# A gated mix of a state-space scan and a long convolution: pair 7 in the plain form, a tile of pair 6 ahead of the last inverse, two of C's sums by DMA, the last row by halves

## The chip, the cores and the metric

The kernel runs on one core of one Trainium2 chip. The metric is device time in microseconds of one execution, as the median of several runs. A core has TensorE (PE, matrix products into PSUM), VectorE (DVE), ScalarE (ACT), GpSimd (POOL) and SyncE (SP), each with its own queue of instructions that it takes in order; DMA transfers are issued from the queues of SP and POOL (a few at the start from ACT) and run on 16 shared DMA engines. An engine waits for another, or for a transfer, on semaphores.

## The reference

Inputs are in bfloat16: a sequence x of 2048 rows and 1024 columns, a diagonal complex state model (1024 states), k and v of the same shape as x, a four-tap filter and a long filter of 2048 taps for each column.

```python
def _A_ref(x, Lambda_re, Lambda_im, B_re, B_im, C_re, C_im, log_dt, Dskip):
    Lam_bar = jnp.exp(dt * Lam)
    B_bar = ((Lam_bar - 1.0) / Lam)[:, None] * Bmat
    Bu = jnp.einsum("bld,pd->blp", x + 0j, B_bar)
    ...
    for t in range(L):
        h = Lam_bar[None, :] * h + Bu[:, t, :]
    ...
    y = 2.0 * jnp.einsum("blp,dp->bld", hseq, Cmat).real + x * Dskip[None, None, :]

def _B_ref(q, k, v, shift_k, ssm_k, ssm_D):
    for t in range(ks):
        k_shift = k_shift + k_pad[:, t:t + S, :] * shift_k[:, ks - 1 - t][None, None, :]
    kv = k_shift * v
    ...
    y_f = kv_f * kf_f[None, :, :, :]
    ...
    y = y + kv * ssm_D[None, None, :]
    return q * y
...
g = _sigmoid((x * gate_w).sum(-1, keepdims=True))
a = _A_ref(x, Lambda_re, Lambda_im, B_re, B_im, C_re, C_im, log_dt, Dskip)
b = _B_ref(x, B_k, B_v, B_shift_k, B_ssm_k, B_ssm_D)
return g * a + (1 - g) * b
```

`kv_f` and `kf_f` are transforms of kv and of the long filter, padded to 4096; `y` is transformed back and cut to 2048 rows, a causal convolution along the sequence.

## The kernel before

**Two halves that overlap.** The first part, to about 212 us, is the convolution. It goes over eight channels c (128 columns each): the four taps and the product with v, transforms of the filter and of kv as matmuls with cosine and sine tables (`fwd_K`, `fwd_V`), their products on VectorE (`products`, tile G), and the transform back (`inverse`: two halves of 8 matmuls into `psz`, each copied by ScalarE to `cv` and stored by SP to a scratch in DRAM, `cv_scr`). In the last channel (lines 1088 to 1116) `products` sums on VectorE alone.

The second part is the state model. Time is cut into 4 blocks tb of 512 rows, the states into 4 groups g of 256 (two sub-groups j of 128). A *pair* i is one (tb, g), in the order of the list `order` (line 671): pairs 4 and 5 are (2, 0) and (2, 1), pair 6 is (0, 2), pair 7 is (0, 3), pair 8 is (1, 2), and so on. For each pair `Bu(i)` makes two tiles, one for each j. The scans then run over pairs of time steps: an even-step input V and an odd-step input U, where V must also hold lam (the complex pole) times the input of the step before.

**Two forms of a tile.** `Bu_tile` (line 710) makes 16 matmuls of 256 columns for the odd steps (`odd`), copies them to U on ScalarE, 16 for the even steps (`even`), and then, after a `yield`, adds lam times the shifted odd steps into the same PSUM with four matmuls against diagonal matrices (`lamd`, made by `lam_diag` from six scaled copies of the identity); for tb > 0 four matmuls of one column are added. `Bu_plain` (line 736) makes 16 matmuls of 512 columns (`both`) for odd and even steps at once and copies them out as they are; `turn_U` (line 750) then adds lam times the shifted odd steps in two parts: ScalarE scales into a tile Q (2 instructions of 512 columns in the first part, 4 of 256 in the second), and a DMA issued by POOL adds Q into V (`gather`). Both parts add into the same V, so the second sum is issued only after the first has landed. Pairs 4, 5 and 8 to 15 are plain; pairs 0 to 3, 6 and 7 have diagonal products.

**The scans and C.** `scan` (line 761) does one pair on VectorE: A from the table times U's V part, two sums, four scan instructions W, hb from W (the even states), then U += lam * hb (the odd states). `advance(j)` runs scan j and already starts scan j + 1 within it. Each of the eight tiles CT of C (`turn_C`, line 1070) must be turned by a complex factor: ScalarE makes two scaled copies m (`m<-CT`), VectorE scales CT twice and adds m (`CT<-CT,m`, 2048 columns). They are done in pairs after scans 0 to 3: CT0 and CT1, CT2 and CT3, and so on.

An output row tile t (128 rows of the output) is `Cy`: for g = 0 to 3, `Cy_g` (line 850) makes 8 matmuls of 512 columns into two PSUM banks, the left and right halves dh of the 1024 columns; rows 0 and 1 of a block read hb, rows 2 and 3 read U. `psy` is the PSUM tile. The convolution's row is loaded from `cv_scr` (`pbb`), scaled by 1 - g on ScalarE, summed with g times Dskip by a DMA of POOL (`pbb<-gd`), multiplied with x on VectorE (`product`), and added to the scaled state part by another DMA (`combine`) or, in the last four rows, on VectorE (`finish`). Row 15 is finished in two halves of 512 columns.

**What sets the order.** Every engine's order is the order in which the program records its instructions (`put` chains each to the one before it on its engine). So generators and lists written out by hand set it: `step(gen)` records the next piece of a generator; `plan` (line 1162) says which tiles of `Bu` (`B8`) and which rows (`C0`) stand behind each scan; `turned` (line 1163) says behind which scan `turn_U` of a pair is recorded; `on_act` holds scalings of CT that are slipped in between tiles. PSUM has four buffers of two banks (`tag="ps"`), used in turn, so a tile of matmuls needs the copies of the fourth tile before it to be done. Pool `Q` has four buffers. DMA transfers of one queue are issued in order, so a store that waits on ScalarE holds back the loads recorded behind it.

Around the change the order on TensorE is: both tiles of pairs 4 and 5 and the gate of block 2, tile 0 of pair 6 (odd, even), first half of the last inverse, tile 0's diagonal products, second half of the inverse, tile 1 of pair 6, the tiles of pair 7, then B8 to B12 and the first row C0.

Of the kernel before, what the change touches and what calls it, by code (L numbers as in the profile page):

```python
# [9 lines left out]
ALU = mybir.AluOpType  # L10
ACT = mybir.ActivationFunctionType
BF16 = mybir.dt.bfloat16
# [8 lines left out]
def kernel(  # L21
# [26 lines left out]
    nc = tc.nc  # L48
# [4 lines left out]
    S, D = xf.shape  # L53
# [5 lines left out]
    NT = S // 128  # L59
# [8 lines left out]
    def pool(name, bufs, **kw):  # L68
        return ctx.enter_context(tc.tile_pool(name=name, bufs=bufs, **kw))
# [6 lines left out]
    lam_pool = pool("lam", 1)  # L76
# [3 lines left out]
    s5p = {"wu": pool("wu", 3)}  # L80
    psum = pool("psum", 4, space=bass.MemoryType.PSUM)

    def u4(shape, dt, name):
        return s5p["wu"].tile(shape, dt, name=name, tag="u4")

    def ps2(shape, name):
        return psum.tile(shape, F32, name=name, tag="ps")
# [4 lines left out]
    def put(eng, f, *a, **kw):  # L92
        with tc.issue_after(prev[eng]) if eng in prev else nullcontext():
            i = f(*a, **kw)  # L94
        prev[eng] = getattr(i, "ins", i)

    def mm(o, l, r, first, last):
        put("pe", nc.tensor.matmul, o, lhsT=l, rhs=r, start=first, stop=last)
# [6 lines left out]
    def tt(o, a, b, op):  # L105
        put("dve", V.tensor_tensor, out=o, in0=a, in1=b, op=op)

    def ts(o, a, s1, s2, op0, op1=None):
        if op1 is None:
            put("dve", V.tensor_scalar, out=o, in0=a, scalar1=s1, scalar2=None, op0=op0)  # L110
        else:
            put("dve", V.tensor_scalar, out=o, in0=a, scalar1=s1, scalar2=s2, op0=op0, op1=op1)
# [4 lines left out]
    def act(o, i, **kw):  # L117
        put("act", nc.scalar.activation, out=o, in_=i, **kw)
# [7 lines left out]
    def gather(o, i):  # L126
        put("pool", nc.gpsimd.dma_start, out=o, in_=i, accum_op=ALU.add)
# [111 lines left out]
    def flat(ap):  # L239
        return ap.rearrange("p a b -> p (a b)")  # L240
# [100 lines left out]
    def small(name):  # L341
        return consts.tile([128, NP], F32, name=name)

    rv, rv2, thn, nthn = small("rv"), small("rv2"), small("thn"), small("nthn")
    c2r, mc2r, mc2i = small("c2r"), small("mc2r"), small("mc2i")
# [303 lines left out]
    def gates_of(c4, sums):  # L649
        act(gcols[:, c4], sums, func=ACT.Sigmoid)  # L650
        act(omg[:, c4], sums, func=ACT.Sigmoid, scale=-1.0)

    def gate(tb):
        psg = ps2([128, 2, 512], "p")[:, 0, 0:4]
        for tl in range(4):
            for dt_ in range(ND):
                mm(psg[:, tl:tl + 1], xTs[tb][:, dt_, tl * 128:(tl + 1) * 128], gwb[:, dt_:dt_ + 1],
                   dt_ == 0, dt_ == ND - 1)
        gates_of(slice(tb * 4, tb * 4 + 4), psg)
# [15 lines left out]
    def lam_diag(g, home, on_act=False):  # L675

        t = lamd[g] = home.tile([128, 2, 3, 128], BF16, name=f"lamd{g}", tag=f"lamd{g % 2}")
        for j in range(2):
            for k, f in enumerate((lam[:, 0], lam[:, 1], mlam)):
                pi = 2 * g + j  # L680
                if on_act:
                    act(t[:, j, k], ident, func=ACT.Identity, scale=f[:, pi:pi + 1])
                else:
                    ts(t[:, j, k], ident, f[:, pi:pi + 1], None, ALU.mult)

    def Bu(i):
        tb, g = order[i]
        if i in (10, 11):
            if i == 10:
                s5p["u2"] = xt_pool.tile([128, 2, 2 * (4 * HB + 4)], BF16, name="U2", tag="xT")  # L690
            U = s5p["u2"][:, i - 10]
        else:
            shape = [128, 2 * (4 * HB + 4)]
            if i in (6, 7, 8, 15):
                U = u4(shape, BF16, "U")
            else:
                home = uu[0 if i in (0, 1, 13, 14) else 1] if i < 6 or i in (13, 14) else s5p["uu"]
                U = home.tile(shape, BF16, name="U")
        if i in (4, 5) or i >= 8:
            V_, O_ = U[:, 0:4 * HB], U[:, 4 * HB:]  # L700
            V_ = V_.rearrange("p (c j t) -> p c j t", c=2, j=2)
            O_ = O_.rearrange("p (c j t) -> p c j t", c=2, j=2)
            Us[tb, g] = V_, O_[:, :, :, 2:]
            turns_U[i] = turn_U(g, V_, O_)
            return [Bu_plain(tb, g, V_, O_, j) for j in range(2)]
        U = U[:, 0:8 * HB].rearrange("p (a c j t) -> p a c j t", a=2, c=2, j=2)
        Us[tb, g] = U[:, 0], U[:, 1]
        return [Bu_tile(tb, g, U, j, (i, j) == (2, 1)) for j in range(2)]
# [26 lines left out]

    def Bu_plain(tb, g, V_, O_, j):
        xT = xTs[tb]
        if j == 0:
            act(O_[:, :, :, 1], ends[:, 1 - tb % 2, g], func=ACT.Copy)
        ps = ps2([128, 2, 2, HB], "both")  # L740
        for c in range(2):
            for dt_ in range(ND):
                mm(flat(ps[:, c]), BT[g][:, c, dt_, j * 128:(j + 1) * 128], xT[:, dt_], dt_ == 0, dt_ == ND - 1)
        act(O_[:, :, j, 2:], ps[:, :, 1], func=ACT.Copy)
        if j == 1 and tb < NTB - 1:
            act(ends[:, tb % 2, g], O_[:, :, :, HB + 1], func=ACT.Copy)
        act(V_[:, :, j], ps[:, :, 0], func=ACT.Copy)
        yield

    def turn_U(g, V_, O_):  # L750
        both = slice(0, 2)
        for part in (((both, both, lam[:, 0]),), ((0, 1, lam[:, 1]), (1, 0, mlam))):
            Q = s5p["Q"].tile([128, 2, 2, HB], BF16, name="Q")
            for j in range(2):
                pi = 2 * g + j
                for c, o, f in part:
                    act(Q[:, o, j], O_[:, c, j, 1:1 + HB], func=ACT.Identity, scale=f[:, pi:pi + 1])
            gather(V_, Q)
            yield
# [90 lines left out]
    def Cy_g(tb, tl, ps, g, last):  # L850
        X = hbs[tb, g] if tl < 2 else Us[tb, g][1]
        tsl = slice(tl % 2 * 128, tl % 2 * 128 + 128)
        for j in range(2):
            for c in range(2):
                for dh in range(2):
                    mm(ps[dh], X[:, c, j, tsl], CT[2 * g + j][:, c, dh * 512:(dh + 1) * 512],
                       g == 0 and j == 0 and c == 0, last and j == 1 and c == 1)

    def a_room(t_):
        if t_ < NT - 8:  # L860
# [43 lines left out]
    def step(gen):  # L904
        next(gen, None)

    def run(gen):
        for _ in gen:
            pass

    def steps(gen, n):
        for _ in range(n):
            step(gen)
# [141 lines left out]
    c = NC - 1  # L1055
    CT = {}
# [11 lines left out]
    m_pool = pool("m", 2, side="right")  # L1068

    def turn_C(pi):  # L1070
        m = m_pool.tile([128, 2, D], BF16, name="m")
        for c in range(2):
            act(m[:, c], CT[pi][:, 1 - c], func=ACT.Identity, scale=mc2i[:, pi:pi + 1])
            yield
        for c, f in enumerate((c2r, mc2r)):
            ts(CT[pi][:, c], CT[pi][:, c], f[:, pi:pi + 1], None, ALU.mult)
        tt(CT[pi], CT[pi], m, ALU.add)

    turning = [turn_C(pi) for pi in range(NP)]
    load_CT(0)  # L1080
# [7 lines left out]
    with tc.tile_pool(name="fin", bufs=1, side="right") as fin:  # L1088

        count = iter(range(16))  # L1090

        def room(shape, dt, name):
            return fin.tile(shape, dt, name=name, tag=f"fin{next(count)}")

        prod, back = products(c, 0, room, False), inverse(c - 1)
        run(old)
        steps(prod, 3)
        run(back)
        b0, b1, b2, b3 = tiles
        run(b0)  # L1100
        gate(1)
        run(b1)
        run(prod)
        lam_diag(2, lam_pool, True)
        run(b2)
        lam_diag(3, lam_pool, True)
        run(b3)
        gate(2)
        steps(turning[0], 2)
        b6, b7 = Bu(6)  # L1110
        step(b6)
        back = inverse(c)
        step(back)
        step(b6)
        run(back)
        steps(turning[1], 2)
    h3.close()
# [18 lines left out]
    def end_late():  # L1136
        while late:
            step(late.pop())

    def filler():  # L1140
        if on_act:
            on_act.pop(0)()

    def Bu_next(i, tiles_=None):
        for b in tiles_ or Bu(i):
            step(b)
            filler()
            end_late()
            filler()
            late.append(b)  # L1150
# [10 lines left out]
    NS = NTB * NG  # L1161
    plan = ["B8", "B9 B10", "B11", "B12 C0", "C1", "C2", "C3", "B13 B14", "C4 B15", "C5", "C6", "C7", "C8", "C9", "C10", "C11"]
    turned = dict(zip(range(3, 12), (8, 9, 4, 10, 11, 12, 13, 14, 15)))
    rows = dict(scaled=0)

    def between(j):
# [24 lines left out]
        if 0 < k < NT - 6:  # L1191
            prepare()

    Bu_next(6, [b7])
    Bu_next(7)
    step(scans[0])
    for j in range(NS):
# [24 lines left out]
    tb = NTB - 1  # L1222
    t0 = tb * 4
    pss = []
    for tl in range(4):
        ps = ps2([128, 2, 512], "psy")
# [42 lines left out]
```

## Time and profile before

| | us |
|---|---|
| median of 3 runs | 401.46 (401.43 to 403.51) |
| profiled execution | 401.09 |
| its span | 399.2 |
| TensorE busy | 385.8 |
| VectorE busy | 380.6 |
| ScalarE busy | 278.5 |
| POOL busy | 65.3 |
| last channel's products on VectorE | 189.4 to 212.4 |
| first half of the last inverse starts on TensorE | 212.54 |
| tile 1 of pair 6 on TensorE (odd, even) | 216.43 to 219.92 |
| first output row starts on TensorE | 262.75 |
| last instruction of VectorE ends | 396.4 |

All times inside an execution are from the start of the span. TensorE's granted clock was 0.998 over the span. In the rows of the profile all instructions that go through a helper have its line (L94), so they are told apart by their tiles: `psz<-G,CI` is written into psz from G and the table CI. The number behind an `x` is a count of merged instructions, the time in front is that of the whole group, and square brackets hold the idle time before it and what ended that. A DMA issued by POOL is busy there only while it is issued (0.86 us for most sums of 256 KB); its landing is a time of its own (median 5.2 us from issue for `U<-Q`, 6.1 for `pbb<-gd`).

### The profile page before, as it was taken

The page shows a single profiled execution, that of the slowest core. Times are in us where ns is not written, and L with a number is a line of the kernel's source. Part 1 is how long each engine was busy: PE and PEld are TensorE (multiplying, and loading weights), DVE is VectorE, ACT ScalarE, POOL GpSimd, SP SyncE. Part 2 cuts the span into 40 slices and gives each one's busy share as a digit, 9 for nine tenths or more (in the row PEclk, how much of TensorE's full clock was granted, in tenths as well). Part 3 has the DMA queues.
Part 4 walks back from the last instruction along what each step waited for, and adds up shares of the span by engine and source line. Part 5 has one row for each costly group of instructions (what it writes and reads, how often), then busy time and mean ns, then how long its engine had stood idle before and what let it go on. Part 6 is the DMA issues. An engine that isn't in the chain of part 4 may idle for free.

```text
span 399.2 us, 6689 instructions
## 1 busy us (share of the span) xinstructions
PE 385.8 (97%) x2499; PEld 214.1 (54%) x2533; DVE 380.6 (95%) x618; ACT 278.5 (70%) x420; POOL 65.3 (16%) x88
## 2 busy tenths in 40 slices
PE   7999899999999999999998999999999999999995
PEld 4556357474656648566455844444444444444442
DVE  8699999999999999998999989999999999999994
ACT  5797986969878796765385379956996568974001
POOL 3011030200202020010000000013433324532100
PEclk9999999999999999999999999999999999999999
DMA  7879994997929397076994999177999879998412
GB/s 160 159 147 229 193 253 78 217 227 133 214 66 221 58 181 163 28 145 96 179 219 130 171 186 172 28 158 126 231 187 197 166 161 214 209 243 195 95 35 107
DMA packets 128451, 63.64 MB, mean 159 GB/s; under 512 B 106265, under 2 KB 113185, under 8 KB 128418
## 3 DMA queue, kind: packets, MB, share of 16 engines
q1 hardware_dynamic: 117664, 42.22, 49.1%
q0 software_dynamic: 10672, 20.98, 30.1%
q8 instruction: 20, 0.33, 0.3%
q14 instruction: 13, 0.11, 0.1%
q10 hardware_dynamic: 82, 0.02, 0.0%
HBM read 12.86 MB, written 8.39 MB: 53 GB/s over the span
## 4 chain that ended last, share of the span: by engine, by line
PE 74%; DVE 14%; ACT 5%; issue 3%; DMA 1%; SPq 1%; another core or an unknown queue 1%; DVEq 0%; ACTq 0%
PE psy L94 27%; PE both L94 14%; PE psk L94 9%; PE even L94 5%; PE taps L94 5%; PE psz L94 5%; PE odd L94 4%; DVE BT L94 4%; DVE wkh L94 4%; PE foldk L94 3%; DVE G L94 3%; ACT Vh L94 3%; PE psv L94 3%; DVE t L94 3%; DMA kn<-in_B_ssm_k_dram 1%
## 5 line engine op out<-in xcount | busy, mean ns | idle before, releaser
L94 PEld LDWEIGHTS <-BT 128*128 128x128 bf16 x704 | 68.5, 98 | 41.9
L94 PE MATMUL both<-xT,BT 128*128 128x512 bf16 x312 | 69.6, 379 | 0.4
L94 PE MATMUL psy<-CT,hb 128*128 128x512 bf16 x251 | 56.3, 379 | 0.3
L94 PE MATMUL psy<-CT,U 128*128 128x512 bf16 x251 | 56.0, 379 | 0.2
L94 PEld LDWEIGHTS <-U 128*128 128x128 bf16 x256 | 25.0, 98 | 30.2
L94 PEld LDWEIGHTS <-hb 128*128 128x128 bf16 x256 | 24.9, 98 | 30.0
L94 ACT ACTIVATE Vh<-psv 128x1024 bf16<-128x1024 f32 x32 | 31.0, 1034 | 11.5 <-PE psv L94 9.7
L94 ACT ACTIVATE U<-both 128x512 bf16<-128x512 f32 x40 | 22.0, 594 | 15.5 <-PE both L94 15.4
L94 DVE TENSOR_TENSOR_SCAN W<-rv,init,A 128x256 bf16<-128x256 f32 x48 | 32.2, 733 | 0.0
L94 PE MATMUL taps<-dg,kT 128*128 128x128 bf16 x512 | 30.5, 220 | 0.7 <-DMA kT<-in_B_k_dram 0.7
L94 PEld LDWEIGHTS <-kT 128*128 128x128 bf16 x512 | 29.1, 98 | 1.8 <-DMA kT<-in_B_k_dram 1.1
L94 PEld LDWEIGHTS <-SF 128*128 128x128 bf16 x192 | 18.8, 98 | 19.8 <-issue 0.6
L94 PE MATMUL psk<-eok,SF 128*128 128x384 bf16 (+1 forms) x126 | 29.0, 352 | 0.3
L94 POOL DMA_DIRECT2D G<-wkh x8 | 9.7, 1218 | 115.2 <-DVE wkh L94 115.2
L94 PE MATMUL psz<-G,CI 128*128 128x512 bf16 x64 | 24.3, 380 | 3.9 <-DVE G L94 3.4
L94 ACT ACTIVATE BT<-psy,gcols 128x1024 bf16<-128x1024 f32 x5 | 5.6, 1113 | 29.3 <-PE psy L94 29.2
L94 PE MATMUL psz<-G,SI 128*128 128x512 bf16 x64 | 24.3, 379 | 0.0
L94 DVE TENSOR_TENSOR U<-U,q 128x512 bf16<-128x512 bf16 (+2 forms) x51 | 23.5, 489 | 0.6
L94 ACT ACTIVATE Q<-U,lam 128x512 bf16<-128x512 bf16 (+1 forms) x40 | 23.1, 605 | 0.0
L94 PE MATMUL even<-xT,BT 128*128 128x256 bf16 x192 | 22.9, 273 | 0.0
L94 POOL DMA_DIRECT2D pbb<-gd x8 | 8.2, 1029 | 89.7 <-ACT U L94 80.3
L94 PE MATMUL odd<-xT,BT 128*128 128x256 bf16 x192 | 22.9, 273 | 0.0
(176 smaller groups left out, 792.2 us busy)
## 6 DMA issues: line engine op xcount, KB each, us to landing
U<-Q POOLq DMA_DIRECT2D x20, 256.0 KB, 5.2
G<-wkh POOLq DMA_DIRECT2D x6, 768.0 KB, 8.5
cv_scr<-cv SPq DMA_DIRECT2D x16, 256.0 KB, 2.5
v<-in_B_v_dram SPq DMA_DIRECT2D x3, 1024.0 KB, 10.3
pbb<-cv_scr SPq DMA_DIRECT2D x8, 256.0 KB, 4.6
xr<-in_A_x_dram SPq DMA_DIRECT2D x8, 256.0 KB, 5.0
pbb<-gd POOLq DMA_DIRECT2D x8, 256.0 KB, 6.1
BT<-cv_scr SPq DMA_DIRECT2D x8, 256.0 KB, 5.7
```

The source lines that it names most:

```text
L94: i = f(*a, **kw)
```

## The change

1. Pair 7 gets the plain form: `Bu` picks `Bu_plain` for it; at tb = 0 there is no earlier block, so POOL writes zeros in place of the copied last odd step; `lam_diag(3)` is gone; `turned[0] = 7` records its `turn_U` around B8, behind scan 0 (first part ahead of B8's tiles, second part behind them).
2. The odd and even matmuls of tile 1 of pair 6 stand ahead of the last inverse, right behind tile 0's. Tile 0's diagonal products now come before the inverse's first half, tile 1's between its halves. Pair 7's two tiles follow the inverse directly.
3. `turn_C` for CT4 and CT5: ScalarE's scaled copies go into two tiles of pool Q, VectorE scales CT twice, and two DMA sums issued by POOL, one for each component, add them. The VectorE sum of 2048 columns is gone for these two.
4. For row 15, each group's 8 matmuls are sorted by half: four into the left half, then four into the right.

```diff
-        if i in (4, 5) or i >= 8:
+        if i in (4, 5, 7) or i >= 8:
...
-        if j == 0:
+        if j == 0 and tb > 0:
             act(O_[:, :, :, 1], ends[:, 1 - tb % 2, g], func=ACT.Copy)
+        elif j == 0:
+            put("pool", nc.gpsimd.memset, O_[:, :, :, 1], 0.0)
...
-        for j in range(2):
-            for c in range(2):
-                for dh in range(2):
-                    mm(ps[dh], X[:, c, j, tsl], CT[2 * g + j][:, c, dh * 512:(dh + 1) * 512],
-                       g == 0 and j == 0 and c == 0, last and j == 1 and c == 1)
+        steps_ = [(j, c, dh) for j in range(2) for c in range(2) for dh in range(2)]
+        if tb * 4 + tl == NT - 1:
+            steps_.sort(key=lambda s_: s_[2])
+        for j, c, dh in steps_:
+            mm(ps[dh], X[:, c, j, tsl], CT[2 * g + j][:, c, dh * 512:(dh + 1) * 512],
+               g == 0 and j == 0 and c == 0, last and j == 1 and c == 1)
...
     def turn_C(pi):
-        m = m_pool.tile([128, 2, D], BF16, name="m")
+        by_sum = pi in (4, 5)
+        if by_sum:
+            m = [s5p["Q"].tile([128, D], BF16, name="Q") for c in range(2)]
+        else:
+            whole_m = m_pool.tile([128, 2, D], BF16, name="m")
+            m = [whole_m[:, c] for c in range(2)]
         for c in range(2):
-            act(m[:, c], CT[pi][:, 1 - c], func=ACT.Identity, scale=mc2i[:, pi:pi + 1])
+            act(m[c], CT[pi][:, 1 - c], func=ACT.Identity, scale=mc2i[:, pi:pi + 1])
             yield
         for c, f in enumerate((c2r, mc2r)):
             ts(CT[pi][:, c], CT[pi][:, c], f[:, pi:pi + 1], None, ALU.mult)
-        tt(CT[pi], CT[pi], m, ALU.add)
+            if by_sum:
+                gather(CT[pi][:, c], m[c])
+        if not by_sum:
+            tt(CT[pi], CT[pi], whole_m, ALU.add)
...
         run(b2)
-        lam_diag(3, lam_pool, True)
         run(b3)
         gate(2)
+        b6, b7 = Bu(6)
+        step(b6)
         steps(turning[0], 2)
-        b6, b7 = Bu(6)
+        step(b7)
         step(b6)
         back = inverse(c)
         step(back)
-        step(b6)
+        step(b7)
         run(back)
         steps(turning[1], 2)
...
+    turned[0] = 7
...
-    Bu_next(6, [b7])
     Bu_next(7)
```

(In these lines b6 and b7 are tiles 0 and 1 of pair 6.)

## The prediction, made blind

> **What bounds the kernel now.** I read the page's first part, then TensorE's waits from 212.6 us to the end, then the chain of waits around 212 us and at the end, then VectorE's instructions in order of time.
>
> ```profile
> PE 385.8 (97%) x2499; PEld 214.1 (54%) x2533; DVE 380.6 (95%) x618; ACT 278.5 (70%) x420; POOL 65.3 (16%) x88
> ```
> Two engines are nearly full, so the stage decides. TensorE's waits after 212.6 us are one row:
>
> ```profile
> engine line waited for: us in total, times, longest us
> PE psz L94 <- DVE G L94: 1.4, 1, 1.4
> ```
> Its place, in the order of instructions on TensorE:
>
> ```profile
> 209.21 1.91 PE L94 MATMUL even<-xT,BT 128*128 128x256 bf16 x16
> 212.54 0.38 PE L94 MATMUL psz<-G,CI 128*128 128x512 bf16 x1 [1.43 <-DVE G L94]
> ```
> So before 212.5 VectorE's products of the last channel (G) set the time, and from there to about 394.8 TensorE does: every matmul saved there is worth its full time, as long as VectorE keeps ahead. How far ahead it is, VectorE's own rows tell (CT is the output matrix that C's rows are multiplied with, A the start of a scan):
>
> ```profile
> 238.81 0.49 DVE L94 TENSOR_SCALAR CT<-CT,c2r 128x1024 bf16<-128x1024 bf16 x1 [1.50 <-ACT m L94]
> ...
> 246.02 0.68 DVE L94 TENSOR_TENSOR A<-TCS,U 128x1024 bf16<-128x1024 bf16 x1
> ...
> 250.78 1.23 DVE L94 TENSOR_TENSOR CT<-CT,m 128x2048 bf16<-128x2048 bf16 x1
> ...
> 266.41 1.23 DVE L94 TENSOR_TENSOR CT<-CT,m 128x2048 bf16<-128x2048 bf16 x1
> ```
> The last sum, CT7, ends at 267.64. TensorE's output rows begin at 262.75 and run at 13.82 us for 64 matmuls, 0.216 each; CT7 is first read by the 29th, at 268.79. VectorE's lead is 1.15 us. The same slack comes back for row 8: scan 11's hb is summed by 343.51 and read by the 25th matmul after 339.53, at 344.71. At the last rows it is over 3 us. Four diagonal products of pair 7 and the end itself, in the chain of waits:
>
> ```profile
> 231.40 0.44 PE even L94 x4
> ...
> 391.58 1.12 ACT BT L94
> ...
> 393.33 1.28 DVE BT L94
> 394.61 0.35 another core or an unknown queue
> 394.98 0.75 DVE BT L94
> 395.73 0.66 DVEq L1264
> ```
> VectorE ends row 14 at 394.61 and waits 0.35 for row 15's first half, whose last matmul is the last but one of all.
>
> **The moved tile.** Tile 1 of pair 6 (32 matmuls of 256 columns, 216.43 to 219.92: 3.49 us) now runs at 211.12, where TensorE waited 1.43. G is ready at 212.4 as before, since nothing that feeds it moves, and the inverse starts at 211.12 + 3.49 + 0.43 (tile 0's diagonal products) = 215.04. Gain 1.43, whole, as the tile covers the gap with 2.06 to spare. Its PSUM needs the copies of pair 5's last tile and of gate 2, which ended at 208.4. Behind it the last inverse ends at 218.93 instead of 216.43, so its copy and its store leave 2.4 later, and so does all that stands behind that store on SP's queue: loads of row 0, Dskip, CT4 to CT7, rows 1 and 2, xT of block 3. The DMA engines, full until 248.5, are then full until about 251, with 3.3 more for two sums of 256 KB (768 KB land in 8.5, 256 KB in 5.2). xT is queued ahead of row 2's two loads and is first read at 253.5 (my time for B12); CT4 is wanted by ScalarE at 241 and lands by 230 (issued at 222.66, 2.4 later now, 4.9 to land). ScalarE's scaling for CT1 moves from 219.6 to 222.2; VectorE takes it at 224.1. Cost nothing; if xT came last of all, up to 0.8.
>
> **Pair 7 in the plain form.** Eight diagonal products go, 0.44 for each four in the chain of waits: 0.87. 64 matmuls of 256 columns become 32 of 512: 2 x 3.49 against 2 x 3.45 (290.38 to 304.19 is four such tiles), 0.08. The six lamd copies (0.39 each) go from ScalarE at 202 to 206, off the path. Added are six ScalarE copies into Q (1.33 + 1.60 us by the rows at 261.48 and 270.87), two sums by DMA, and one POOL memset (110 ns by kT's row) that lies idle time before. ScalarE has room: it was idle 2.81 at 231.50. By my times: pair 7's tiles end at 225.84; copies 1.22, Q's first part 1.33, sum one is issued at 228.4. B8's tiles end at 229.29 and 232.74; copies and the scalings for CT2 and CT3 (2.17 each) take ScalarE to 236.2, Q's second part to 237.8, where sum two is issued. CT3's scaling was done at 238.8 before; now VectorE reaches it at 237.31 and does not wait: VectorE gains the 1.50 of the row above.
>
> The new wait: scan 3's A (246.02 less 1.50 = 244.52) now needs sum two. The sum for row 0 that POOL issued at 241.15, amid the same loads, landed in 6.0. In the list of DMA issues 256 KB sums land in 3.3 to 9.0 (medians of their groups), so it lands at 241.1 to 246.8; I take 6.0, 243.8: no wait. At 9.0 VectorE waits 2.3. Behind A stand all later scans. POOL holds row 0's sum behind sum two; its product is due at 250.6, and it lands by about 246 to 250.
>
> **C's two sums by DMA.** Two VectorE sums of 1.23 go: 2.45. VectorE's lead over TensorE at CT7 and at row 8 becomes 1.15 + 1.50 + 2.45 - 2.38 (what TensorE gains) = 2.72. Without these savings it would be -1.23, and TensorE would wait; so they earn no term but keep the others. The four DMA sums stand on POOL behind row 1's, which follows ScalarE at 251.3; issues of 0.86 from 252.2, the last landing at 252.2 + 5.2 + 3 x 1.65 (3.3 per 512 KB) = 262.4. TensorE reads the last at 260.37 + 22 matmuls = 265.1. Even at 9.0 after its issue it is there at 263.8. ScalarE's scaling for CT5 waits for sum two to free its Q, due 245.4, landed 243.8.
>
> **The last row.** Row 15's left half is done four matmuls early, so VectorE goes from 394.61 to it without the 0.35: it starts at about 394.65, and the right half, complete at 394.8, follows. Gain between 0 and 0.37; I take 0.33.
>
> **Sum**: 1.43 + 0.87 + 0.08 + 0.33 = 2.71. The profiled execution took 401.09 (span 399.2 and 1.9 around it) and becomes 398.4; the median of the runs, 401.46, lies 0.37 above it, so I predict 398.7. A change within 0.5%, 2.0 us, can't be told from none.
>
> **Rivals.**
> (a) Sum two is late. It costs TensorE time only from 244.52 + 2.72 = 247.24, 9.4 us after its issue. For it: the DMA share is above 1.0 from 225 to 245. Against it: 6.0 in just that stretch. At 10.4 it costs 1.0, time 399.7; at 12, 401.3. The Trainium skill (DMA: Bandwidth & Descriptors, Anatomy of one DMA — SWDGE (gpsimd) path) fits 2.0 us and a microsecond per 436 KB to such a transfer, an estimate of 2.6 us here; by it neither (a) nor (b) could happen and the sum would stand as it is. The rows are twice that, so both keep their chance.
> (b) Slower: both sums are late. POOL may not issue sum two before sum one has landed (in before, 2.33 us of such a wait stand at 290.34). With a landing of L each, the second lands at 228.4 + 2L once L is over 9.4; the gain is used up at 249.95, L = 10.8. At L = 12 it lands at 252.4, TensorE waits 5.2, and the time is 403.9. For it: DMA engines that are full for the whole stretch. Against it: no median of a 256 KB sum is over 9.0.
> (c) POOL's issues hold VectorE: six more of 0.86 are 5.2 us; less the lead of 2.72, TensorE waits 2.4: 401.1. Against it: the two A sums at 241.60, while POOL issued, took 0.76, as at 255.18 with POOL idle. The Trainium skill (GPSIMD Engine Reference, Key points) says that GpSimd shares its SBUF interfaces with VectorE and contends with VectorE instructions with two SBUF inputs; this row shows none of it.
> (d) The move does not do what it says: G slips by 2.06 or more, or PSUM holds the tile back, and the 1.43 comes back: 400.1.
>
> **Chances.** Forecast 0.66 (its own range 398.2 to 399.3); better than it, below 398.2, 0.03; (a) 0.13; (b) 0.09; (c) 0.04; (d) 0.05. Faster by over 0.5% (below 399.45) is the first two and 0.01 of (a): 0.70. Slower by over 0.5% (above 403.5) is (b) and 0.01 of (a): 0.10. The rest of (a), (c) and (d), 0.20, is no change. The range of 397.9 to 400.6 holds the forecast, (d) and most of (a), about 0.8; its upper end is a landing of 11.3 for sum two, beyond the 9.0 that the rows bound.
>
> **What would show it.** Right: TensorE has no wait for G at the last inverse, which starts near 215.0; first output row near 260.4; no wait for CT3 on VectorE; scan 3's A near 244.5; VectorE's two half rows at the end without a gap. Wrong: an idle time on VectorE before scan 3's A with a DMA as releaser, or on TensorE before CT4 to CT7, or on POOL between the two sums for pair 7 well past 237.8.

## The result, and the profile after

| | before | changed |
|---|---|---|
| median, us | 401.58 (401.38 to 403.94, 9 runs) | 399.37 (398.94 to 401.06, 9 runs) |
| ratio | | 0.9939, 95% interval 0.9918 to 0.996 |
| span of the profiled execution, us | 399.2 | 397.3 |
| tile 0 of pair 6 (`even`) to first output row, us | 53.54 | 51.01 |
| first output row to the end of VectorE's last instruction, us | 133.64 | 133.64 |

The change is 2.2 us faster; 2.7 were forecast. The last two rows of the table cut the execution from 209 us on into two stretches, and they tell almost everything that follows: the first stretch is from the start of the `even` matmuls of pair 6's tile 0 (209.21 before, 209.54 after) to the start of the first `psy` matmul (262.75, 260.55), the second from there to the end of the last VectorE instruction (396.39, 394.19). All of the gain, 2.53, is in the first, and the last row's reordering, which lies in the second, gained nothing. The span fell by less, 1.9, since two parts that lie outside the stretches were longer in this profile: the one ahead of 209 us by 0.33, and the one from VectorE's last instruction to the end of the span by 0.30 (2.84 before, 3.14 changed). The second of these is scatter: two runs below with the same end have 2.88 and 2.89.

The page's first part for the changed kernel:

```profile
PE 387.4 (97%) x2493; PEld 210.8 (53%) x2493; DVE 378.3 (95%) x616; ACT 279.4 (70%) x420; POOL 70.8 (18%) x95
```

VectorE has two instructions fewer (the two sums of C), POOL is busy 5.5 us more (pair 7's two issues of 0.86, C's four with 3.81 together, and the memset). TensorE's list of waits from 203 us to the end is empty, where the wait for G stood. Its instructions in order of time (start, duration, count, and in brackets the idle time before):

```profile
211.29 1.91 PE L94 MATMUL odd<-xT,BT 128*128 128x256 bf16 x16
213.03 1.91 PE L94 MATMUL even<-xT,BT 128*128 128x256 bf16 x16
214.78 0.60 PE L94 MATMUL even<-U,lamd 128*128 128x255 bf16 x4
215.22 0.38 PE L94 MATMUL psz<-G,CI 128*128 128x512 bf16 x1
...
260.55 13.98 PE L94 MATMUL psy<-CT,hb 128*128 128x512 bf16 x64
```

The moved tile stands at 211.29, the inverse follows at 215.22 with no bracket, and the first row at 260.55. VectorE in the same order, with the three places at which the forecast could have failed:

```profile
237.51 0.48 DVE L94 TENSOR_SCALAR CT<-CT,c2r 128x1024 bf16<-128x1024 bf16 x1
...
244.71 0.68 DVE L94 TENSOR_TENSOR A<-TCS,U 128x1024 bf16<-128x1024 bf16 x1
...
262.57 1.23 DVE L94 TENSOR_TENSOR CT<-CT,m 128x2048 bf16<-128x2048 bf16 x1
...
391.13 1.28 DVE L94 SCALAR_TENSOR_TENSOR BT<-psy,gcols,xlast 128x1024 bf16<-128x1024 f32 x1
392.78 1.41 DVE L94 SCALAR_TENSOR_TENSOR BT<-psy,gcols,xlast 128x512 bf16<-128x512 f32 x2 [0.37 <-PE psy L94]
```

CT3's scaling and scan 3's A start without an idle time. CT7 is done at 263.80; the 29th matmul of row 0, which reads it first, is due at 260.55 + 28 x 0.216 = 266.59, so VectorE's lead there is 2.79. Row 15's left half, in the last line, still waits 0.37. POOL's queue:

```profile
229.11 0.86 POOL L94 DMA_DIRECT2D U<-Q  x1 [49.59 <-ACT U L94]
238.47 0.86 POOL L94 DMA_DIRECT2D U<-Q  x1 [8.50 <-DMA CT<-in_A_C_im_dram]
...
252.22 3.81 POOL L94 DMA_DIRECT2D CT<-Q  x4
```

In the list of DMA issues the two sums of pair 7 landed 4.3 and 5.1 after their issue, and C's four 5.8 in the median. Sum one was there at 233.4, so it did not hold sum two, which waited for ScalarE's second part of Q. (The releaser named in the bracket is only the event that came last; in two runs below the same row names `ACT Q`.) Sum two landed at 243.6, 1.1 before A.

The chain of waits at the end:

```profile
316.74 76.01 PE psy L94 x352
392.75 0.03 issue
392.78 0.75 DVE BT L94
393.53 0.66 DVEq L1276
```

Both half rows stand behind TensorE's last matmul, 0.75 and 0.66, just as before.

### The profile page after: what moved, and what is told of

Same layout as the page of the kernel before. It is cut to its first block, busy times and chain, and to the rows that moved or that the text cites. A ratio compares the mean times of both kernels' runs of the same rounds, so it can differ in the third digit from the quotient of the medians.

```text
span 397.3 us, 6652 instructions
## 1 busy us (share of the span) xinstructions
PE 387.4 (97%) x2493; PEld 210.8 (53%) x2493; DVE 378.3 (95%) x616; ACT 279.4 (70%) x420; POOL 70.8 (18%) x95
## 4 chain that ended last, share of the span: by engine, by line
PE 82%; DVE 9%; ACT 6%; issue 2%; POOL 0%; DVEq 0%; POOLq 0%; ACTq 0%
PE psy L94 28%; PE both L94 19%; PE psk L94 9%; PE psz L94 5%; PE taps L94 5%; PE even L94 5%; PE odd L94 4%; DVE BT L94 3%; PE psv L94 3%; PE foldk L94 3%; ACT Vh L94 2%; DVE wkh L94 2%; DVE G L94 1%; PE p L94 1%; DVE t L94 1%
## 5 line engine op out<-in xcount | busy, mean ns | idle before, releaser
L94 PEld LDWEIGHTS <-BT 128*128 128x128 bf16 x672 | 65.4, 98 | 45.2
L94 PE MATMUL both<-xT,BT 128*128 128x512 bf16 x352 | 76.8, 379 | 0.0
L94 ACT ACTIVATE U<-both 128x512 bf16<-128x512 f32 x44 | 24.2, 594 | 17.3 <-PE both L94 17.2
L94 POOL DMA_DIRECT2D U<-Q x22 | 19.2, 942 | 89.7 <-ACT U L94 51.8
L94 PE MATMUL psk<-eok,SF 128*128 128x512 bf16 (+1 forms) x128 | 29.4, 352 | 0.0
L94 ACT ACTIVATE Q<-U,lam 128x512 bf16<-128x512 bf16 (+1 forms) x44 | 25.5, 607 | 0.0
L94 DVE TENSOR_TENSOR wkh<-BT,Vh 128x3072 bf16<-128x3072 bf16 (+4 forms) x20 | 21.8, 1111 | 0.0
L94 DVE TENSOR_TENSOR wkh<-Kh,Vh 128x3072 bf16<-128x3072 bf16 (+2 forms) x16 | 21.3, 1352 | 0.0
```

## The experiments

Eight kernels ran in two groups of four, each group on one chip with runs of the kernel before; each ratio is to those (median 401.37 in the first group, 401.36 in the second).

| run | median, us | ratio to before (95%) | tile 0 to first row, us | first row to end, us |
|---|---|---|---|---|
| moved tile alone | 399.75 | 0.9960 (0.9948 to 0.9973) | 51.96 | 133.64 |
| pair 7 alone | 400.39 | 0.9979 (0.9970 to 0.9988) | 52.59 | 133.64 |
| changed, C's sums back on VectorE | 398.87 | 0.9943 (0.9930 to 0.9957) | 51.01 | 133.63 |
| changed, four VectorE instructions more | 401.04 | 0.9990 (0.9981 to 0.9999) | 51.01 | 135.64 |
| changed, again | 399.54 | 0.9947 (0.9929 to 0.9966) | 51.01 | 133.64 |
| changed, row 15 in the old order | 399.23 | 0.9940 (0.9924 to 0.9957) | 51.01 | 133.64 |
| changed, row 15's halves in two PSUM tiles | 398.76 | 0.9930 (0.9914 to 0.9946) | 51.00 | 132.98 |
| changed, left half and two right quarters | 398.15 | 0.9917 (0.9898 to 0.9936) | 51.00 | 132.75 |

The medians scatter by some tenths, the two stretches repeat to 0.01; differences under 0.5 us are read from the stretches.

### The moved tile alone

```diff
--- before
+        b6, b7 = Bu(6)
+        step(b6)
         steps(turning[0], 2)
-        b6, b7 = Bu(6)
+        step(b7)
         step(b6)
         back = inverse(c)
         step(back)
-        step(b6)
+        step(b7)
         run(back)
...
-    Bu_next(6, [b7])
```

> The kernel before with the moved tile alone (tile 1 of pair 6 ahead of the last inverse; pair 7 with its diagonal products, C's sums on VectorE and row 15's order as before). My theory: TensorE's idle time before the last inverse was the whole price there, and TensorE sets the time from that point on, so the time falls by the idle time itself, 1.4 to 1.6 us, to about 400.0; TensorE shows no wait for G, the first output row starts 1.4 to 1.6 earlier than 262.75, and VectorE's wait of 1.50 for CT3 shrinks to under 0.2, so that its lead over TensorE stays near 1.1. Rival (the gap comes back: G slips, or VectorE's lead of 1.15 is used up by the 1.5): a gain of at most 1.15, and TensorE waits in front of the 29th matmul of row 0 or at row 8.

1.62 us less by the medians, 1.58 in the first stretch, none in the second. TensorE:

```profile
214.77 0.60 PE L94 MATMUL even<-U,lamd 128*128 128x255 bf16 x4
215.21 0.38 PE L94 MATMUL psz<-G,CI 128*128 128x512 bf16 x1
```

and VectorE at CT3, where before there was a wait of 1.50:

```profile
236.35 1.23 DVE L94 TENSOR_TENSOR CT<-CT,m 128x2048 bf16<-128x2048 bf16 x1
237.56 0.49 DVE L94 TENSOR_SCALAR CT<-CT,c2r 128x1024 bf16<-128x1024 bf16 x1
```

So the gap before the inverse was paid in full, and filling it returned 1.58, not the 1.43 that the bracket showed. The difference is in how the profile draws a matmul's end, which it models: the `even` matmuls of pair 6's tile 0 start at 209.21 and end, as drawn, at 211.11, but in the changed kernel the next ones start 1.75 after them (209.54 to 211.29), 0.16 before the drawn end of 1.91. Here a wait read off against a drawn end is short by that much. The wait for CT3 went by itself: ScalarE's scaling follows TensorE's tiles, and it ended at 237.53 in place of 238.78. VectorE gets its time back when TensorE stops being late.

### Pair 7 alone

```diff
--- before
-        if i in (4, 5) or i >= 8:
+        if i in (4, 5, 7) or i >= 8:
...
-        lam_diag(3, lam_pool, True)
...
+    turned[0] = 7
```

(with the zeros for tb = 0 as in the change.)

> The kernel before with pair 7 in the plain form alone (no moved tile, C's sums on VectorE, row 15's order as before). My theory: 0.87 for the eight diagonal products and 0.08 for the wider matmuls, 0.95 in all, to about 400.6; TensorE's wait of 1.43 for G stays; scan 3's A has no wait on a DMA. Rival (the two sums come late, or the six issues on POOL hold VectorE, and it is C's sums by DMA that paid for it): a gain of 0.3 or less, with TensorE waits in front of the products with CT7 or at row 8.

0.98 by the medians, 0.95 in the first stretch: the forecast's 0.87 + 0.08 to the hundredth. TensorE's wait of 1.42 for G stays, as it should:

```profile
209.32 1.91 PE L94 MATMUL even<-xT,BT 128*128 128x256 bf16 x16
212.65 0.38 PE L94 MATMUL psz<-G,CI 128*128 128x512 bf16 x1 [1.42 <-DVE G L94]
```

VectorE's A of scan 3 starts without a wait at 245.17. Of VectorE's wait of 1.50 for CT3 0.61 is left, about what TensorE's 0.95 leaves of it. The two edits add up: 1.58 + 0.95 = 2.53, which is the changed kernel's 53.54 - 51.01.

### C's sums back on VectorE

```diff
--- changed
-        by_sum = pi in (4, 5)
+        by_sum = False
```

> The changed kernel with C's two sums put back on VectorE (two of 1.23, 2.45 us more on VectorE before the last CT). My theory: VectorE's lead over TensorE in the changed kernel is 2.79 at CT7 and 2.39 at row 8; less 2.45 it is 0.33 and about -0.06, so TensorE waits 0.0 to 0.1 and the time is the changed kernel's within 0.3 us (399.1 to 399.7): C's DMA sums bought reserve and no time. Rival (VectorE sets the time in this stretch, each microsecond of it counts): 2.45 more, 401.8.

No time lost: 0.9943 against 0.9939 and 0.9947 for the changed kernel, and the same two stretches. VectorE's CT7 and scan 11's hb for row 8:

```profile
265.37 1.22 DVE L94 TENSOR_TENSOR CT<-CT,m 128x2048 bf16<-128x2048 bf16 x1
...
342.01 0.75 DVE L94 TENSOR_TENSOR hb<-hb,trn 128x512 bf16<-128x512 bf16 x2
```

CT7 is ready at 266.59 and due at 260.86 + 6.04 = 266.90: 0.31 of lead left, 0.33 expected. hb is ready at 342.76; row 8 started at 337.63 and reads it with its 25th matmul, at 342.81: 0.05 left. So in the changed kernel C's sums buy only reserve, and the forecast's "so they earn no term but keep the others" is not borne out. Its -1.23 is 1.15 - 2.38, without C's 2.45 and without the 1.50 at CT3; but the 1.50 comes from TensorE's earlier tiles and stays when C's sums go: 1.15 + 1.50 - 2.38 = 0.27, against the 0.31 of this run. (The median, 398.87, is a little below the range expected, the ratio is not.)

### Four VectorE instructions more

```diff
--- changed
         if not by_sum:
+            if pi >= 6:
+                for _ in range(2):
+                    tt(whole_m, whole_m, whole_m, ALU.max)
             tt(CT[pi], CT[pi], whole_m, ALU.add)
```

> The changed kernel with four idle VectorE instructions of 1.23 us added (maximum of CT6's and CT7's summand with itself, twice each; 4.92 us, results unchanged). My theory: VectorE's lead takes the first 2.4 and the rest is TensorE's wait: 4.92 less 2.79 = 2.1 us of waiting in front of the products with CT7, and about 0.4 more at row 8, 2.5 in all, time 401.9. Rival 1 (VectorE sets the time, no lead): 4.9 more, 404.3. Rival 2 (VectorE has far more room than I read): no change, 399.4.

VectorE and TensorE around CT7:

```profile
260.31 2.48 DVE L94 TENSOR_TENSOR m<-m 128x2048 bf16<-128x2048 bf16 x2
...
264.76 2.48 DVE L94 TENSOR_TENSOR m<-m 128x2048 bf16<-128x2048 bf16 x2
267.27 1.23 DVE L94 TENSOR_TENSOR CT<-CT,m 128x2048 bf16<-128x2048 bf16 x1
```

```profile
260.50 6.21 PE L94 MATMUL psy<-CT,hb 128*128 128x512 bf16 x28
268.55 7.93 PE L94 MATMUL psy<-CT,hb 128*128 128x512 bf16 x36 [1.84 <-DVE CT L94]
```

Counted from the first output row, CT7 comes 8.00 later where it came 3.25 later, so the four cost VectorE 4.75. TensorE stands for 268.55 - (260.50 + 6.04) = 2.01 (the bracket says 1.84, short by the drawn end again), and the second stretch is 2.00 longer, by the ratios the time is 1.7 to 2.1 more. So 2.74 of 4.75 was free, where 2.79 of lead was read. The rivals (4.9 more, or nothing) are off by 2.9 and 2.0 us. The 0.4 more at row 8, part of the 2.5 expected, did not come: hb was ready at 344.33 and due at 339.27 + 5.18 = 344.45. VectorE had made up 0.47 on the way, for a reason that stands in the last section.

### Row 15 in the old order

```diff
--- changed
-        if tb * 4 + tl == NT - 1:
-            steps_.sort(key=lambda s_: s_[2])
```

> The changed kernel with row 15's matmuls in the old order (left and right half in turn). My theory: the new order does nothing, since both halves lie in one PSUM tile and TensorE tells VectorE of that tile once, after its last matmul; the time is the changed kernel's within 0.2 us, and VectorE's first half row of row 15 starts 1.65 after row 14's (row 14 at 391.13, row 15 at 392.78 in the changed kernel) in either order. Rival (the prediction's step: the left half is released four matmuls early): 0.33 us slower than the changed kernel, and the wait of 0.37 for psy longer than in the changed kernel.

VectorE's last two lines, first of the changed kernel run again, then with the old order:

```profile
392.38 1.28 DVE L94 SCALAR_TENSOR_TENSOR BT<-psy,gcols,xlast 128x1024 bf16<-128x1024 f32 x1
394.03 1.41 DVE L94 SCALAR_TENSOR_TENSOR BT<-psy,gcols,xlast 128x512 bf16<-128x512 f32 x2 [0.37 <-remote]
```

```profile
390.54 1.28 DVE L94 SCALAR_TENSOR_TENSOR BT<-psy,gcols,xlast 128x1024 bf16<-128x1024 f32 x1
392.19 1.41 DVE L94 SCALAR_TENSOR_TENSOR BT<-psy,gcols,xlast 128x512 bf16<-128x512 f32 x2 [0.37 <-remote]
```

1.65 from row 14 to row 15 and a wait of 0.37 in both: the order within the group does nothing. It was not for want of time: in the changed kernel TensorE ends at 392.75, the left half's last matmul stands four matmuls of 0.216 earlier and so ends at about 391.9, and VectorE is free at 392.41; yet it starts at 392.78, behind the last matmul of all.

### Row 15's halves in two PSUM tiles

```diff
--- changed
+    left = ps2([128, 512], "psy")
...
+        Cy_half(left, g, 0)
...
+    Cy_half(left, NG - 1, 0)
+    right = ps2([128, 512], "psy")
+    halves.append((slice(512, 1024), right))
+    for g in range(NG):
+        Cy_half(right, g, 1)
+    run(fins[3])
```

`Cy_half` makes the four matmuls of one half for one group; row 15 is no longer among the rows that `Cy_g` makes.

> The changed kernel with row 15's two halves in PSUM tiles of their own: the left half is finished with the last group as before, and the right half's 16 matmuls all stand at the very end, in the tile that row 12 leaves free. The matmuls are the same in number and size. My theory: VectorE is told of the left half 16 matmuls (3.4 us) before the end, takes it there, and after the last matmul only one half row is left: 0.66 to 0.75 less than the changed kernel, no wait for row 14's copy. Rival (the end is not VectorE's two half rows but the last store, or TensorE waits for row 12's tile): within 0.2 of the changed kernel, or slower.

```profile
388.55 1.94 DVE L94 SCALAR_TENSOR_TENSOR BT<-psy,gcols,xlast 128x1024 bf16<-128x1024 f32 x2
392.79 0.75 DVE L94 SCALAR_TENSOR_TENSOR BT<-psy,gcols,xlast 128x512 bf16<-128x512 f32 x1 [2.30 <-remote]
```

Row 14 and the left half now run back to back (two instructions in the first line, the second of 512 columns), 2.30 before the right half, and one half row is left after TensorE's end: 0.66 less in the second stretch, as expected. The matmuls are the same in number and size, but order and tile changed together, as the right half's 16 now all stand last. That an order within one tile is not enough, the run before shows; no run kept one tile with the right half's 16 at the end.

### A half and two quarters

```diff
--- with the halves in two tiles
-    right = ps2([128, 512], "psy")
-    halves.append((slice(512, 1024), right))
-    for g in range(NG):
-        Cy_half(right, g, 1)
+    for lo in (512, 768):
+        part = ps2([128, 256], "psy")
+        halves.append((slice(lo, lo + 256), part))
+        for g in range(NG):
+            Cy_cols(part, g, lo, 256)
```

> As the run with the halves apart, but the right half split once more into two PSUM tiles of 256 columns (32 matmuls of 256 columns in place of 16 of 512). My theory: after the last matmul a quarter row is left, about 0.4 in place of 0.75, and the matmuls cost 0.05 to 0.1 more (3.49 against 3.45 for a tile of them): 0.2 to 0.3 less than with the halves apart, 0.9 to 1.0 less than the changed kernel. Rival (the end's fixed part or the more numerous stores take it back): no less than with the halves apart.

```profile
391.25 0.48 DVE L94 SCALAR_TENSOR_TENSOR BT<-psy,gcols,xlast 128x256 bf16<-128x256 f32 x1 [0.59 <-PE psy L94]
392.99 0.48 DVE L94 SCALAR_TENSOR_TENSOR BT<-psy,gcols,xlast 128x256 bf16<-128x256 f32 x1 [1.26 <-PE psy L94]
```

The first quarter goes 1.74 before the second, one tile of 16 matmuls of 256 columns earlier. The second stretch is another 0.23 shorter, 0.89 less than in the changed kernel. This is the fastest version that ran: 398.15, 0.9917 of the time before (0.9898 to 0.9936); by the stretches it is 2.54 + 0.89 = 3.43 us ahead of the kernel before, by the medians 3.2.

## Why the prediction held, point by point

- **What bounds the kernel.** Right. From 209 us to its last matmul, TensorE's time is the kernel's: whatever was taken from its row came out at the end, 1.58 and 0.95 alone and 2.53 together.
- **The moved tile, 1.43.** Right in mechanism, small by 0.15, which is the drawn end of a matmul. Forecast for the inverse's start 215.04, measured 215.22; G ended 0.33 later than before, with the whole first part of the kernel, and the tile covered it. The store that the forecast has "leave 2.4 later" is 2.5 later by its own figures (218.93 - 216.43); the first load behind it on SP's queue was issued 2.68 later (219.87, 222.55), and neither TensorE nor VectorE waited for a load, as forecast.
- **Pair 7, 0.87 and 0.08.** Right: 0.95 measured by itself. Sum two was forecast to be issued at 237.8 and landed at 243.8; it was issued at 238.47 and landed at 243.6. The Trainium skill (DMA: Bandwidth & Descriptors, Anatomy of one DMA — SWDGE (gpsimd) path) fits 2.0 us and a microsecond per 436 KB to it, an estimate of 2.6 us; 4.3, 5.1 and a median of 5.8 were measured among full DMA engines, and the measurement decides.
- **C's two sums, no term.** Right as a term. That the others needed them was wrong, as shown above: 0.31 and 0.05 us of lead are left without them.
- **The last row, 0.33. This is the step that failed**: "VectorE goes from 394.61 to it without the 0.35". It measured 0 (133.64 before, changed, and with the order undone). The order of the matmuls was taken for the time of the release. In the built program's instructions TensorE raises its semaphore for this group once, by 8 and with the last of its matmuls; the left half row waits for that count, and the right one stands behind it. The semaphore events in the changed kernel's trace agree: TensorE's comes at 391.03 for row 14, and then at 392.75 alone. With tiles of their own the parts have events of their own: at 389.31 for the left half apart, at 391.22 for the first of the two quarters.
- **The sum.** 1.58 + 0.95 + 0 = 2.53 against 2.71: the 0.33 that never came, less the 0.15 that the gap was larger. The two misses have opposite signs, so that the sum came nearer than its worst term; that is luck. The median of 399.37 is 0.67 above the forecast of 398.7, and 0.07 above the forecast's own range of 398.2 to 399.3. The terms account for 0.18 of that; the rest lies in what stands outside the two stretches, which scatters: by the medians the changed kernel gained 2.21 here and 1.82 when it ran again.
- **The rivals.** (a) and (b), late sums: the margin was 1.1 before A and 2.8 of lead behind it, so the landing of 5.1 could have been 9.0; neither happened. The run with four instructions more shows what a later VectorE costs, its delay less the lead, which is how both rivals were priced; a late sum itself was not tried. (c), POOL's issues hold VectorE: not at A's sums (0.76 again, at 240.28 beside an issue at 240.54), but elsewhere by a little, below. (d): the moved tile alone rules it out.

## What to carry to other kernels

Cut the execution at a few fixed instructions and compare the stretches between them: they repeat to 0.01 us where medians scatter by some tenths, and each edit shows in its own stretch. Here VectorE was released by its whole PSUM tile, so to let a half go early give it a tile of its own, and make the last piece behind the last matmul small. Before spending DMA issues to free an engine, work out its lead with and without all the other edits: an engine that was waiting for the one you speed up gets that wait back.

## What the runs showed of the hardware that was not expected

**The first load made one execution slow.** The changed kernel and the one with the old order are the same program up to the last row, yet their profiled executions took 400.46 and 398.65. The tile at 209 us is already 1.84 later in the first (210.79 against 208.95). TensorE's wait for the first load of the filter, in the first kernel and then in the second:

```profile
PE foldk L94 <- DMA kn<-in_B_ssm_k_dram: 2.3, 1, 2.3
```

```profile
PE foldk L94 <- DMA kn<-in_B_ssm_k_dram: 0.7, 1, 0.7
```

1.6 of the 1.84 is this one transfer. It does not explain all of the scatter: in the other eight profiles this wait is 1.4 or less and the tile starts at 209.21 to 209.85, not in the order of the waits (0.9 goes with 209.21, no listed wait with 209.72).

**POOL's issues lengthen one form of VectorE instruction.** VectorE's scalings q of hb, from 263 to 345 us (smallest, median and largest duration in ns), first in the changed kernel, then with four instructions more:

```profile
L94 DVE TENSOR_SCALAR q<-hb,lam x32: 334/350/460, 271.4 to 340.9; 128x512 bf16<-128x512 bf16 x32
```

```profile
L94 DVE TENSOR_SCALAR q<-hb,lam x31: 335/348/368, 276.1 to 344.9; 128x512 bf16<-128x512 bf16 x31
```

In the changed kernel a group of four takes 1.14 us, but 1.22 to 1.28 in four cases, each beside a DMA issue of POOL, such as 310.46 (1.28) beside an issue at 310.50. In the run with four instructions more VectorE's groups fell elsewhere against POOL's issues and all seven whole groups took 1.14 or 1.15. The four excesses are 0.44 together: the 0.47 that VectorE made up there. Over all ten profiles from 263 to 350 us, the 22 whole groups without an issue beside them all took 1.14; of the 58 with one, 28 took 1.18 to 1.37. The single records of the traces tell which: of 321 scalings 30 took over 375 ns, and 26 of these started 0.20 to 0.31 us after the start of an issue and ended 0.68 or 0.69 after it, whenever they had started; only one other scaling started in that window. So they were held to a fixed point of the issue. Sums with two inputs took 0.75 to 0.76 for a pair with or without an issue beside them, and those that started in the same window took 415 to 424 ns each, as elsewhere. The Trainium skill (GPSIMD Engine Reference, Key points) names both two-input instructions and those in a two-port performance mode as contending with GpSimd; the first is not seen here, and no run shows which mode the scalings are in. Rival (c) was thus a real effect of 0.4 us in 80, and it lay within the lead.
